# Tile 0's and tile 1's slots chosen anew: load order, ScalarE's slots and the places of VectorE's weight sums

## Chip, cores and metric

One core of a Trainium2 chip. The metric is the device time of one execution in microseconds (us); smaller is better. Times are medians of several executions; all the comparisons below use executions at the full granted clock ("fast"), and where one fell into a throttled state it is said.

## The reference

Eight batches of eight heads of linear attention (576 positions, head size 64), then a mixture of four experts over all 4608 tokens, each expert a product 512 to 1024, a ReLU and a product 1024 to 512, weighted by normalised probabilities.

```python
def phi(x):
    return np.where(x > 0, x, np.exp(x) - 1.0) + 1.0
q_p, k_p = (phi(q), phi(k))
kv = np.einsum('bhsd,bhse->bhde', k_p, v)
z = np.sum(k_p, axis=2)
num = np.einsum('bhsd,bhde->bhse', q_p, kv)
den = np.einsum('bhsd,bhd->bhs', q_p, z)[..., None] + 1e-06
# ... (num / den, heads laid side by side: x)
for e in range(E):
    h = np.maximum(x @ w1[e], 0.0)
    out += p[:, e:e + 1] * (h @ w2[e])
```

## The kernel before

The expert products are done in half-size blocks in the manner of Strassen and Winograd: seven products in place of eight, for which sums of weights, of tokens and of h are needed. The sums of weights are made once, in tile 0 and tile 1, by VectorE, in fp16, 128x1024 each. The sums of h are made in every unit (one tile and one expert) by GpSimd, 128x512 each. The loads go through one queue in the order of a list. Every piece of work has a slot, a number; the slots are sorted and the instructions issued in that order. In the traces here each engine runs its instructions in that order, so a slot decides what stands behind what.

```python
    "DMA": ('w100', 'w101', 'w102', 'w103', 'w200', 'lk1', 'w201', 'w110', 'w111', 'k0', # ... (cut)
    "WS2": ((1.0, 9.5, 29.0, 27.5), (14.5, 32.2, 38.5, 50.9), (70.95, 80.2, 92.75, 79.8), (60.3, 85.95, 92.75, 81.2)),
# ... (cut: weight_sums for w1, slots WS1, L605 to L613, is of the same kind)
    def weight_sums2(e, part):                       # VectorE, both inputs in SBUF: L620, L622, L624, L626
        # ... (cut)
        if part == 0:
            nc.vector.tensor_tensor(out=tw[:, 0], in0=b12, in1=b11, op=AO.subtract)
        elif part == 1:
            nc.vector.tensor_tensor(out=tw[:, 1], in0=b22, in1=tw[:, 0], op=AO.subtract)
        elif part == 2:
            nc.vector.tensor_tensor(out=tw[:, 2], in0=b21, in1=tw[:, 1], op=AO.subtract)
        else:
            nc.vector.tensor_tensor(out=b12, in0=b22, in1=b12, op=AO.subtract)

    def hidden_sum(h, hs, i):                        # GpSimd: L635, L637, L639, L641
        # ... (cut)
        if i == 0:
            nc.gpsimd.tensor_tensor(out=hs[0], in0=a21, in1=a22, op=AO.add)
        elif i == 1:
            nc.gpsimd.tensor_tensor(out=hs[1], in0=hs[0], in1=a11, op=AO.subtract)
        # ... (cut: i == 2 and i == 3 likewise)

    def add_acc(j, e, ns, ps, ds, first):            # frees a PSUM bank that TensorE waits for
        # ... (cut)
        if first:
            nc.scalar.activation(acc, ps, AF.Identity, scale=pscal)             # L568
        else:
            nc.vector.scalar_tensor_tensor(                                      # L570
                out=acc, in0=ps, scalar=pscal, in1=acc, op0=AO.mult, op1=AO.add
            )

    # of the attention of the next batch, on the same PSUM buffers by turns (aps):
    # left_dve (VectorE, L367) reads psum_el and writes qlp; pe_xl (TensorE, L404) then takes that bank as psum_xl;
    # dma_qT (a transposing transfer issued by SyncE) writes qT; nd (TensorE, L465) reads it
# ... (cut)
        for fj, pos in enumerate(CFG["L1P"]):
            put_at(pos, group, fj)
        # ... (cut)
            for i in range(4):
                put_at(CFG["WS1"][e][i], weight_sums, e, i)
                put_at(CFG["WS2"][e][i], weight_sums2, e, i)
        # ... (cut)
        work.sort(key=lambda w: w[0:2])
        for _, _, g in work:
            g[0](*g[1:])
```

Of the kernel before, what the change touches and what calls it, by code (L numbers as in the profile page):

```python
# [17 lines left out]


CFG = {  # L20
    "DMA": ('w100', 'w101', 'w102', 'w103', 'w200', 'lk1', 'w201', 'w110', 'w111', 'k0', 'w120', 'w121', 'v0', 'w210', 'lk0', 'w211', 'lv1', 'k1', 'k2', 'lv0', 'v1', 'w131', 'w130', 'v2', 'k3', 'v3', 'q1', 'q0', 'w220', 'w221', 'q2', 'q3', 'w230', 'w231'),
    "BLK": (-5.0, 2.0, 10.5, 18.5, 28.0, 36.0, 56.0),
    "L1P": (-69.15, -64.1, -39.9, -36.2, -35.4, -24.38, -16.38, -16.08),
    "L2P": ((-14.38, -14.35, -14.33, -13.58, -11.58, -11.51, -11.2, -10.2, -9.5, -4.0, -2.0, 2.45, 2.45, 2.55, 13.55, 16.5), (17.5, 18.7, 18.9, 19.4, 20.95, 21.6, 22.1, 22.2, 26.4, 26.45, 28.55, 30.95, 31.25, 31.3, 34.75, 37.0), (35.75, 38.05, 41.2, 42.0, 43.45, 43.6, 43.6, 43.6, 45.35, 46.05, 47.1, 48.6, 53.95, 55.0, 58.45, 59.1), (54.55, 56.3, 56.4, 58.6, 61.3, 61.4, 63.3, 63.5, 64.1, 64.1, 66.3, 66.89, 70.95, 70.95, 78.25, 78.5)),
    "TS0": (-52.15, -46.1, -23.38, -16.97),
    "WS1": ((-2.0, 1.95, 40.0, 16.05), (-16.88, -10.13, -2.0, -2.2), (7.85, 12.0, 14.95, 10.0), (25.1, 25.38, 33.64, 31.0)),
    "WS2": ((1.0, 9.5, 29.0, 27.5), (14.5, 32.2, 38.5, 50.9), (70.95, 80.2, 92.75, 79.8), (60.3, 85.95, 92.75, 81.2)),
    "ATTN": (
        dict(
            v=(18.3, 24.16, 28.05, 31.12),  # L30
            k=(-2.05, 25.8, 28.0, 28.5),
            kd=(-1.0, 26.5, 29.8, 30.7),
            lv=19.5,
            lk=14.7,
            lkd=15.45,
            kv=(33.8, 34.3),
            q=(34.9, 36.95, 39.2, 41.7),
            qd=(38.25, 38.4, 41.95, 43.6),
            lq=54.05,
            lqd=56.5,  # L40
            qt=(41.6, 43.8, 45.2, 45.4),
            nd=(45.45, 45.55, 46.1, 47.35),
            xt=(50.15, 53.7, 53.95, 55.1),
            qtl=58.23,
            nl=70.95,
            xl=89.22,
            next=(-3.0, -2.05, 33.69, 40.65, 45.2, 45.55),
        ),
        dict(
            v=(4.4, 8.7, 12.1, 14.8),  # L50
            k=(0.3, 2.9, 6.7, 11.25),
            kd=(7.1, 3.84, 14.3, 14.8),
            lv=10.36,
            lk=9.9,
            lkd=11.6,
            kv=(17.5, 19.1),
            q=(20.1, 22.1, 27.0, 30.0),
            qd=(21.75, 27.2, 30.2, 32.3),
            lq=33.9,
            lqd=38.3,  # L60
            qT=35.9,
            nd=(39.3, 40.4, 42.0, 43.5, 45.3, 46.1),
            nl=52.1,
# [3 lines left out]
    "L2ORD": (2, 5, 1, 6, 3, 7, 4),  # L67
    "L2AT": (3.9, 5.0, 5.8, 7.0, 7.2, 8.4, 9.1, 10.3, 12.9, 13.1, 15.1, 15.1, 16.8, 16.8),
    "TSUM": (-6.7, -4.7, -1.6, -0.7),
    "TSUM1": (2.9, 4.1, 6.3, 6.54),  # L70
    "PR": (-20.88, 40.55, 61.5, 52.95),
    "LATE": (4.0, 14.0, 16.0, 24.0),
    "MODE": {'k0': 0, 'q2': 1, 'k3': 0, 'q0': 0, 'k2': 0, 'k1': 1, 'q1': 0, 'q3': 0, 'T3': 0, 'T0': 0, 'T1': 1, 'v1': 2, 'v2': 0, 'v3': 2, 'v0': 0, 'T2': 1},
    "APS": ('s', 'e', 'b', 'py'),
# [953 lines left out]
```

## Time and profile before

| | before |
|---|---|
| time, median of 6 runs (lowest to highest) | 496.37 us (495.51 to 497.09) |
| span of the profiled run, granted clock | 494.2 us, 0.998 |
| TensorE busy, of the span | 483.7 us, 98% |
| VectorE, ScalarE, GpSimd busy | 77%, 68%, 72% |
| time that TensorE's starts lost, by the count of the prediction | 13.13 us, 11.20 of it before 100 us |

"Lost" is how much later a matmul starts than the one before it and its size allow. The prediction below shows the lines of this kernel's profile.

### The profile page before, as it was taken

The page shows a single profiled execution, that of the slowest core. Times are in us where ns is not written, and L with a number is a line of the kernel's source. Part 1 is how long each engine was busy: PE and PEld are TensorE (multiplying, and loading weights), DVE is VectorE, ACT ScalarE, POOL GpSimd, SP SyncE. Part 2 cuts the span into 40 slices and gives each one's busy share as a digit, 9 for nine tenths or more (in the row PEclk, how much of TensorE's full clock was granted, in tenths as well). Part 3 has the DMA queues.
Part 4 walks back from the last instruction along what each step waited for, and adds up shares of the span by engine and source line. Part 5 has one row for each costly group of instructions (what it writes and reads, how often), then busy time and mean ns, then how long its engine had stood idle before and what let it go on. Part 6 is the DMA issues. An engine that isn't in the chain of part 4 may idle for free.

```text
span 494.2 us, 11615 instructions
## 1 busy us (share of the span) xinstructions
PE 483.7 (98%) x4346; PEld 409.7 (83%) x4346; DVE 378.4 (77%) x802; ACT 336.6 (68%) x678; POOL 355.8 (72%) x341
## 2 busy tenths in 40 slices
PE   9999989999999999999999999999999999999996
PEld 4556656788898989898989898989898888888885
DVE  5657888798867987698859886888688756775686
ACT  6767969964987488848894789468954565446530
POOL 3635204778977797769776977698669877987775
PEclk9999999999999999999999999999999999999999
DMA  9999975552355234633466245522231020002003
GB/s 257 213 219 240 272 138 149 184 121 51 108 190 114 57 111 158 137 67 92 134 166 81 71 150 139 102 57 90 87 73 36 4 96 1 1 2 86 1 1 86
DMA packets 82104, 53.65 MB, mean 109 GB/s; under 512 B 46240, under 2 KB 75808, under 8 KB 82048
## 3 DMA queue, kind: packets, MB, share of 16 engines
q1 hardware_dynamic: 70512, 40.00, 31.2%
q0 software_dynamic: 9888, 11.41, 12.2%
q10 hardware_dynamic: 1648, 1.51, 1.1%
q8 instruction: 34, 0.56, 0.5%
q14 instruction: 22, 0.18, 0.1%
HBM read 45.16 MB, written 9.44 MB: 110 GB/s over the span
## 4 chain that ended last, share of the span: by engine, by line
PE 81%; DMA 10%; DVE 3%; ACT 3%; POOL 1%; issue 1%; DVEq 0%; POOLq 0%; ACTq 0%
PE py L668 38%; PE pb L733 22%; PE pe L733 16%; DMA w<-in_moe_w_dram 7%; DMA rawu<-in_q_dram 2%; PE warm_ps L860 1%; PE psum_nd L465 1%; DMA rawb<-in_v_dram 1%; PE psum_kv L425 1%; DVE acc L570 1%; DVE x_sb L448 1%; PE pb L668 1%; PE py L579 0%; ACT u L744 0%; ACT psum_ee L315 0%
## 5 line engine op out<-in xcount | busy, mean ns | idle before, releaser
L570 DVE SCALAR_TENSOR_TENSOR acc<-py,p_sb,acc 128x256 f32<-128x256 f32 (+1 forms) x382 | 182.3, 488 | 49.5 <-PE py L668 40.2
L717 DVE CUSTOM_DVE_ANT_0 h<-pe,u 128x512 f16<-128x512 f32 x140 | 96.3, 688 | 42.1 <-PE pe L733 27.4
L733 PEld LDWEIGHTS <-w 128*128 128x128 f16 x1120 | 108.8, 98 | 17.5 <-issue 1.7
L635 POOL TENSOR_TENSOR hs<-h 128x512 f16<-128x512 f16 x64 | 74.0, 1156 | 55.2 <-DVE h L717 53.8
L668 PEld LDWEIGHTS <-h 128*128 128x128 f16 x1024 | 99.6, 98 | 11.8 <-issue 0.5
L668 PE MATMUL py<-w,h 128*128 128x256 f16 x744 | 106.4, 273 | 0.0
L744 ACT COPY u<-pb 128x512 f32<-128x512 f32 x140 | 82.7, 591 | 27.7 <-PE pb L733 25.5
L637 POOL TENSOR_TENSOR hs<-hs,h 128x512 f16<-128x512 f16 x64 | 74.7, 1168 | 26.7 <-PE py L668 24.1
L733 PEld LDWEIGHTS <-s 128*128 128x128 f16 x840 | 81.6, 98 | 11.8 <-issue 0.4
L733 PE MATMUL pb<-tt,w 128*128 128x256 f16 x560 | 84.0, 273 | 0.9 <-ACT u L744 0.9
L668 PEld LDWEIGHTS <-hs 128*128 128x128 f16 x768 | 74.4, 98 | 9.9 <-issue 1.2
L641 POOL TENSOR_TENSOR hs<-h,hs 128x512 f16<-128x512 f16 x64 | 74.6, 1166 | 3.5 <-PE py L668 2.9
L668 PE MATMUL py<-t,hs 128*128 128x256 f16 x496 | 74.4, 272 | 0.6 <-DVE acc L570 0.4
L639 POOL TENSOR_TENSOR h<-h 128x512 f16<-128x512 f16 x64 | 74.5, 1165 | 0.0
L759 ACT ACTIVATE h<-pe 128x512 f16<-128x512 f32 x70 | 41.8, 597 | 44.9 <-PE pe L733 44.4
L753 ACT COPY pe<-pb 128x512 f32<-128x512 f32 x70 | 40.3, 575 | 41.6 <-PE pb L733 14.7
L777 ACT ACTIVATE h<-pb 128x512 f16<-128x512 f32 x70 | 41.9, 599 | 9.7 <-PE pb L733 9.5
L733 PE MATMUL pb<-tt,s 128*128 128x256 f16 x280 | 42.0, 273 | 0.1
L733 PE MATMUL pe<-tt,s 128*128 128x256 f16 x280 | 42.0, 273 | 0.0
L733 PE MATMUL pb<-xT,w 128*128 128x256 f16 x248 | 37.2, 273 | 0.3 <-DMA w<-in_moe_w_dram 0.2
L733 PE MATMUL pe<-xT,s 128*128 128x256 f16 x248 | 37.2, 273 | 0.1
L668 PE MATMUL py<-w,hs 128*128 128x256 f16 x248 | 37.2, 273 | 0.0
(121 smaller groups left out, 607.1 us busy)
## 6 DMA issues: line engine op xcount, KB each, us to landing
out_dram<-acc SPq DMA_DIRECT2D x32, 256.0 KB, 2.5
w<-in_moe_w_dram POOLq DMA_DIRECT2D x14, 512.0 KB, 13.1
rawb<-in_v_dram SPq DMA_DIRECT2D x26, 256.0 KB, 2.7
rawb<-in_q_dram SPq DMA_DIRECT2D x26, 256.0 KB, 2.7
rawb<-in_k_dram SPq DMA_DIRECT2D x26, 256.0 KB, 3.1
w<-in_moe_w_dram POOLq DMA_DIRECT2D x4, 256.0 KB, 5.8
rawb<-in_k_dram POOLq DMA_DIRECT2D x4, 256.0 KB, 11.5
rl<-in_q_dram SPq DMA_DIRECT2D x16, 64.0 KB, 2.5
```

The costliest lines, as they stand in the source:

```text
L570: nc.vector.scalar_tensor_tensor(out=acc, in0=ps, scalar=pscal, in1=acc, op0=AO.mult, op1=AO.add)
L635: nc.gpsimd.tensor_tensor(out=hs[0], in0=a21, in1=a22, op=AO.add)
L637: nc.gpsimd.tensor_tensor(out=hs[1], in0=hs[0], in1=a11, op=AO.subtract)
L639: nc.gpsimd.tensor_tensor(out=a21, in0=a11, in1=a21, op=AO.subtract)
L641: nc.gpsimd.tensor_tensor(out=hs[3], in0=a12, in1=hs[1], op=AO.subtract)
L668: nc.tensor.matmul(out=ps, lhsT=lhsT(k), rhs=rhs[:, k], start=first and k == 0, stop=k == FH - 1, skip_group_check=True,)
L717: nc.vector._custom_dve(TENSOR_ADD_SAT, out=out, in0=ps, in1=u, s0=BIG, s1=0.0)
L733: nc.tensor.matmul(out=ps[:, kk], lhsT=lk(kc), rhs=rhs[:, kc], start=first and kk == 0 and kc == 0, stop=kc == 1, skip_group_check=True,)
L744: nc.scalar.copy(u, self.b)
L753: nc.scalar.copy(self.e5, self.b)
L759: nc.scalar.activation(self.h[:, :, 0, 0:NH], self.e5, AF.Relu)
L777: nc.scalar.activation(self.h[:, :, 1, 0:NH], self.b, AF.Relu)
```

## The change

Intent: tile 0's and tile 1's slots are chosen anew, so that loads land when they are needed, and VectorE's sums of weights do not fall on GpSimd's sums of h. No instruction is added, removed or resized.

```diff
-    "DMA": ('w100', 'w101', 'w102', 'w103', 'w200', 'lk1', 'w201', 'w110', 'w111', 'k0', 'w120', 'w121', 'v0', 'w210', 'lk0', 'w211', 'lv1', 'k1', 'k2', 'lv0', 'v1', 'w131', 'w130', 'v2', 'k3', 'v3', 'q1', 'q0', 'w220', 'w221', 'q2', 'q3', 'w230', 'w231'),
-    "BLK": (-5.0, 2.0, 10.5, 18.5, 28.0, 36.0, 56.0),
+    "DMA": ('w100', 'w101', 'w102', 'w103', 'k0', 'w201', 'lk1', 'w200', 'w111', 'w110', 'w121', 'w120', 'lv0', 'lk0', 'w211', 'w210', 'v2', 'v1', 'v0', 'k1', 'w130', 'lv1', 'w131', 'q0', 'k2', 'k3', 'v3', 'w220', 'q2', 'q1', 'w221', 'q3', 'w230', 'w231'),
+    "BLK": (-7.0, 0.5, 9.5, 16.5, 27.0, 36.5, 56.0),
...(cut: L1P, L2P, TS0)
-    "WS1": ((-2.0, 1.95, 40.0, 16.05), (-16.88, -10.13, -2.0, -2.2), (7.85, 12.0, 14.95, 10.0), (25.1, 25.38, 33.64, 31.0)),
-    "WS2": ((1.0, 9.5, 29.0, 27.5), (14.5, 32.2, 38.5, 50.9), (70.95, 80.2, 92.75, 79.8), (60.3, 85.95, 92.75, 81.2)),
+    "WS1": ((13.95, 16.35, 48.05, 14.35), (-20.54, -18.83, -3.5, -0.5), (8.8, 8.95, 15.75, 9.75), (24.56, 28.38, 31.14, 25.8)),
+    "WS2": ((-1.55, 8.26, 33.15, 34.42), (19.45, 32.66, 45.5, 63.9), (73.5, 87.35, 91.2, 82.18), (61.8, 93.5, 104.41, 85.13)),
...(cut: the other slots of batch 1's attention)
-            xl=89.22,
+            xl=95.55,
...(cut: TSUM1, PR)
```

More of the change, by code (lines that the diff above doesn't have):

```diff
@@ L20 @@
 CFG = {
-    "DMA": ('w100', 'w101', 'w102', 'w103', 'w200', 'lk1', 'w201', 'w110', 'w111', 'k0', 'w120', 'w121', 'v0', 'w210', 'lk0', 'w211', 'lv1', 'k1', 'k2', 'lv0', 'v1', 'w131', 'w130', 'v2', 'k3', 'v3', 'q1', 'q0', 'w220', 'w221', 'q2', 'q3', 'w230', 'w231'),
-    "BLK": (-5.0, 2.0, 10.5, 18.5, 28.0, 36.0, 56.0),
-    "L1P": (-69.15, -64.1, -39.9, -36.2, -35.4, -24.38, -16.38, -16.08),
-    "L2P": ((-14.38, -14.35, -14.33, -13.58, -11.58, -11.51, -11.2, -10.2, -9.5, -4.0, -2.0, 2.45, 2.45, 2.55, 13.55, 16.5), (17.5, 18.7, 18.9, 19.4, 20.95, 21.6, 22.1, 22.2, 26.4, 26.45, 28.55, 30.95, 31.25, 31.3, 34.75, 37.0), (35.75, 38.05, 41.2, 42.0, 43.45, 43.6, 43.6, 43.6, 45.35, 46.05, 47.1, 48.6, 53.95, 55.0, 58.45, 59.1), (54.55, 56.3, 56.4, 58.6, 61.3, 61.4, 63.3, 63.5, 64.1, 64.1, 66.3, 66.89, 70.95, 70.95, 78.25, 78.5)),
@@ L25 @@
-    "TS0": (-52.15, -46.1, -23.38, -16.97),
-    "WS1": ((-2.0, 1.95, 40.0, 16.05), (-16.88, -10.13, -2.0, -2.2), (7.85, 12.0, 14.95, 10.0), (25.1, 25.38, 33.64, 31.0)),
-    "WS2": ((1.0, 9.5, 29.0, 27.5), (14.5, 32.2, 38.5, 50.9), (70.95, 80.2, 92.75, 79.8), (60.3, 85.95, 92.75, 81.2)),
+    "DMA": ('w100', 'w101', 'w102', 'w103', 'k0', 'w201', 'lk1', 'w200', 'w111', 'w110', 'w121', 'w120', 'lv0', 'lk0', 'w211', 'w210', 'v2', 'v1', 'v0', 'k1', 'w130', 'lv1', 'w131', 'q0', 'k2', 'k3', 'v3', 'w220', 'q2', 'q1', 'w221', 'q3', 'w230', 'w231'),
@@ new lines @@
+    "BLK": (-7.0, 0.5, 9.5, 16.5, 27.0, 36.5, 56.0),
+    "L1P": (-69.15, -64.1, -39.9, -36.2, -35.4, -23.25, -13.43, -13.43),
+    "L2P": ((-13.38, -13.35, -13.33, -12.08, -10.08, -9.81, -9.2, -8.7, -7.5, -5.5, -2.0, -1.45, -0.5, 8.3, 10.35, 12.55), (14.35, 17.2, 17.2, 17.9, 20.95, 21.1, 21.6, 21.7, 28.0, 28.55, 29.05, 31.45, 31.75, 32.5, 34.25, 37.0), (35.75, 37.97, 42.4, 42.55, 43.05, 44.8, 44.8, 45.55, 46.0, 46.55, 46.75, 48.0, 51.75, 58.0, 58.45, 59.1), (54.25, 56.3, 56.89, 58.2, 59.1, 62.1, 63.6, 63.7, 64.1, 65.9, 66.1, 69.0, 69.95, 70.65, 78.45, 78.5)),
@@ L28 @@
+    "TS0": (-52.15, -46.1, -23.38, 1.0),
+    "WS1": ((13.95, 16.35, 48.05, 14.35), (-20.54, -18.83, -3.5, -0.5), (8.8, 8.95, 15.75, 9.75), (24.56, 28.38, 31.14, 25.8)),
+    "WS2": ((-1.55, 8.26, 33.15, 34.42), (19.45, 32.66, 45.5, 63.9), (73.5, 87.35, 91.2, 82.18), (61.8, 93.5, 104.41, 85.13)),
     "ATTN": (
         dict(
-            v=(18.3, 24.16, 28.05, 31.12),
-            k=(-2.05, 25.8, 28.0, 28.5),
-            kd=(-1.0, 26.5, 29.8, 30.7),
-            lv=19.5,
-            lk=14.7,
@@ L35 @@
-            lkd=15.45,
-            kv=(33.8, 34.3),
-            q=(34.9, 36.95, 39.2, 41.7),
-            qd=(38.25, 38.4, 41.95, 43.6),
-            lq=54.05,
-            lqd=56.5,
-            qt=(41.6, 43.8, 45.2, 45.4),
-            nd=(45.45, 45.55, 46.1, 47.35),
-            xt=(50.15, 53.7, 53.95, 55.1),
-            qtl=58.23,
-            nl=70.95,
-            xl=89.22,
-            next=(-3.0, -2.05, 33.69, 40.65, 45.2, 45.55),
+            v=(18.1, 19.16, 22.55, 30.55),
+            k=(-5.5, 26.3, 27.5, 28.5),
@@ new lines @@
+            kd=(0.5, 27.07, 30.0, 30.7),
+            lv=23.45,
+            lk=15.35,
+            lkd=16.3,
+            kv=(33.6, 34.0),
+            q=(36.4, 36.95, 40.2, 43.4),
+            qd=(37.75, 39.0, 40.55, 44.7),
+            lq=54.05,
+            lqd=54.5,
+            qt=(42.1, 45.0, 45.8, 46.25),
+            nd=(46.7, 47.0, 47.05, 47.8),
+            xt=(48.15, 50.45, 51.45, 54.8),
+            qtl=57.23,
+            nl=71.0,
+            xl=95.55,
+            next=(-0.5, 0.5, 36.3, 44.55, 46.65, 47.45),
@@ L69 @@
     "TSUM": (-6.7, -4.7, -1.6, -0.7),
-    "TSUM1": (2.9, 4.1, 6.3, 6.54),
-    "PR": (-20.88, 40.55, 61.5, 52.95),
+    "TSUM1": (3.76, 4.1, 6.3, 9.92),
+    "PR": (-21.88, 47.0, 56.27, 39.85),
     "LATE": (4.0, 14.0, 16.0, 24.0),
```

## The prediction

> **What bounds the kernel now.** I read the page first, then the time by stages, then TensorE's own timeline, and only then the waits. The stage table (window; its length; busy us and instruction count of PE, PEld, DVE, ACT, POOL; granted clock; share of the DMA engines; GB/s) says most:
>
> ```profile
> 0.00:20.00 20.00, 18.46 (x120) 9.75 (x121) 14.12 (x41) 13.14 (x28) 11.04 (x23) 1.00 1.09 240
> 20.00:60.00 40.00, 38.21 (x258) 23.91 (x257) 26.35 (x48) 31.29 (x62) 15.81 (x23) 1.00 1.17 241
> 60.00:75.00 15.00, 13.65 (x110) 8.60 (x109) 12.88 (x31) 10.26 (x22) 0.99 (x2) 1.00 0.73 142
> 75.00:115.00 40.00, 39.10 (x340) 31.24 (x338) 34.51 (x65) 33.37 (x74) 26.39 (x23) 1.00 0.55 147
> 115.00:480.00 365.00, 365.00 (x3446) 328.35 (x3444) 280.91 (x599) 248.08 (x496) 293.22 (x265) 1.00 0.32 83
> ```
>
> From 115 to 480 us TensorE has no gap. Only tile 0 and the entry into tile 1 can give time back. Busy time flatters TensorE, because the modelled end of a matmul lies some 0.16 us behind the start of the next. So I took starts instead: a 256-column matmul is followed by the next after 109 ns, a 512-column one after 216, a 130-column one after 56, a 128-column one after 55 (medians of the timeline). Whatever a start lies later than that is lost. The loss is 13.1 us in all: 2.9 before 10 us, 1.0 in 10 to 20, **7.8 us in 20 to 120**, about 0.02 per 10 us from there to 480, and 0.6 at the end. The 7.8 us is the whole purse of this change: the order of the first 170 matmuls (up to about 29 us) and of everything from tile 2 on is the same in both kernels.
>
> Who took the 7.8 us (lines of TensorE's timeline: start, us, what, idle time before it and what ended it):
>
> ```profile
> 41.82 0.60 PE L733 MATMUL pb<-tt,w 128*128 128x256 f16 x4 [0.31 <-ACT u L744]
> ...
> 56.78 0.61 PE L579 MATMUL py<-w,h 128*128 128x512 f16 x2 [0.47 <-DMA w<-in_moe_w_dram]
> ...
> 67.10 0.27 PE L465 MATMUL psum_nd<-kvz,qT 128*128 128x130 f16 x2 [0.38 <-ACT qT L416]
> 67.53 0.29 PE L465 MATMUL psum_nd<-kvz,qT 128*128 128x130 f16 x2 [0.15 <-DVE x_sb L448]
> 68.11 0.29 PE L465 MATMUL psum_nd<-kvz,qT 128*128 128x130 f16 x2 [0.30 <-DVE x_sb L448]
> ...
> 98.12 0.60 PE L668 MATMUL py<-t,hs 128*128 128x256 f16 x4 [0.35 <-DVE acc L570]
> ```
>
> By starts: 2.9 us in seven waits before 60 us (ScalarE copies 0.56 and 0.47, the landings of w130 0.41 and w220 0.63, sums and kp on VectorE 0.26, 0.27, 0.33); 2.5 us in 65 to 72 us, where q arrives late and TensorE then waits for each numerator (1.05 us for the copies of qT, 1.44 us for x_sb); 2.1 us in 84 to 112 us; the rest in pieces under 0.1 us.
>
> The sums that the title means are seen on VectorE and on GpSimd:
>
> ```profile
> 93.45 1.46 DVE L626 TENSOR_TENSOR w<-w 128x1024 f16<-128x1024 f16 x1
> 94.84 1.64 DVE L622 TENSOR_TENSOR t<-w,t 128x1024 f16<-128x1024 f16 x1
> 96.40 0.68 DVE L626 TENSOR_TENSOR w<-w 128x1024 f16<-128x1024 f16 x1
> ```
> ```profile
> 93.22 1.15 POOL L639 TENSOR_TENSOR h<-h 128x512 f16<-128x512 f16 x1
> 94.33 1.60 POOL L641 TENSOR_TENSOR hs<-h,hs 128x512 f16<-128x512 f16 x1
> ```
>
> The same sum takes 0.68 us alone and 1.46 or 1.64 us where GpSimd is adding.
>
> **What the Trainium skill says.** "SBUF — State Buffer", section "Who interferes with whom", says that a VectorE instruction with two SBUF inputs takes its second one through the interface that GpSimd reads by, and that the one that issues second is blocked until the first has ended. The trace agrees in kind: the pair above costs VectorE 0.78 and 0.96 us and GpSimd 0.45. The accumulations (one input in PSUM) beside GpSimd keep to 0.47 us. "Perfetto Trace Analysis", section "Identifying the Most-Contended Engine", warns that matmul busy time is no measure of TensorE's headroom; the trace agrees (98% on the page, yet 7.8 us to be had in the first quarter). "DMA: Bandwidth & Descriptors", section "Issuing engines are not separate DMA queues", says that transfers of all issuers share the same engines. Here the queue is full from 14 to 68 us (share over 1), so a new order moves landings without adding bandwidth.
>
> **The change part by part.** No instruction is added, removed or resized: every engine has the same work, and GpSimd's list gets only another order of DMA issues. So the gain is only a matter of waits.
>
> *1. Weight sums away from the sums of h.* In the profile before, four VectorE sums are stretched: 0.92, 1.46, 1.64 and 1.64 us instead of 0.68, together 2.9 us; four GpSimd sums take 1.50, 1.60, 1.48 and 1.60 instead of 1.15, together 1.6 us. Most is off the path. What TensorE lost behind it: 0.52 and 0.12 us at 98 to 99 us (an accumulation queued behind the sums of 93.45 to 97.08), 0.30 at 107.55 (it waited for GpSimd's L639) and 0.12 at 111.5: 1.06 us. In the new order these sums stand apart, and the third sum of expert 3's w2 goes from second in a pair to some 10 us later. I count 0.7 us gained.
>
> *2. The order of the loads.* A 512 KB piece of weights lands 2.5 us after the one before it, a 256 KB piece of q or k after 0.7. New: k0 before w20x, w201 before w200, w111 before w110. Before, w110 landed at 27.55 us and w111 at 30.13, and the first product of expert 1, which reads w110, started at 29.62. Now w110 is the last of this group, and k0 (0.65) is ahead of it: 30.13 + 0.65 = 30.8 us, against a use at 29.65: **1.15 us lost**, new. w200 comes at 25.07 + 0.7 = 25.8, just when layer 2 begins (25.73). This replaces the 0.26 us at 31.6.
>
> *3. Later landings.* The set of pieces up to w121 is equal, so it ends at 35.6 in both. Then w130 comes by about 47.2 (before 50.00), so its wait of 0.41 goes. q1 moves behind w220, so w220 lands by about 55.3 to 56 (before 56.74) and its 0.63 goes. q2 lands by 56 (before 61.66), the last q by 60.5 to 61.5 (before 62.39).
>
> *4. Slots of ScalarE and of expert 1's blocks.* The blocks come closer together, with more TensorE work between a sixth product and the seventh, which needs ScalarE's copy. Of the 0.56 and 0.47 I leave 0.3. k0 to k3 and the last v still tie kv: 0.5 as before. Sum to 57 us: 1.15 + 0.1 + 0.3 + 0.5, with small pieces 2.2 us; before, the start at 57.23 lay 2.96 us behind a run without waits. Gain 0.75.
>
> *5. The passage at 65 to 72 us.* ScalarE is full in 50 to 65 us. Two v casts and one k go earlier, and it no longer waits for q2 (0.55 us before). Of the 1.05 us for qT I leave 0.5 to 0.7. The numerators then stay a chain: eight steps of a reciprocal and a product (0.55 us each) through two PSUM banks, with less TensorE work between them than before (0.9 us against 1.3 in 4 us). I leave 1.9 us where there were 1.44. Net here about 0.
>
> Sum: 0.75 + 0 + 0.7 = 1.45 us, and a little for pieces under 0.1 us: 1.7 us, of 496.5 to **494.8 us**.
>
> **Rivals.** (a) *The new wait for w110 is carried to the end.* For it: it is a landing, which nothing on chip hastens. Against: a delay at 30 us uses up the later waits for landings. If it stays whole and the passage at 65 gets worse, the time is 496.5 to 497.5. (b) *ScalarE is the bound at 75 to 100 us.* It is busy 4.9 of each 5 us there, with the same work in nearly the same order, so an earlier start hits it as new waits for its copies: gain under 0.5 us, 496 us. (c) *All waits for landings and sums vanish.* Without the 7.8 us it would be 488.7; half of it gives 492.6. (d) *The sums are all of it*: 1.06 us, 495.5.
>
> **Range and chances.** Even the whole purse, 7.8 us, is 1.6%: over 2% faster is shut out unless the steady part changes, whose order doesn't. Slower by 2% would need 9.9 us of new waits, and the largest I find is 1.15. So within 2% is nearly certain. The range, 492.6 to 497.0, goes from half of the purse to rival (a).
>
> **What would show it.** Right: VectorE's 128x1024 sums all near 0.68 us and GpSimd's near 1.15; a wait for a landing of w just before the first product of expert 1 near 30 us; none for w near 50 and 56 us; the waits of psum_nd for x_sb still there, about 1.9 us; no change after 120 us except an earlier start. Wrong: stretched sums still there, no wait at 30 us (then the gain is nearer 2.5 us), or new waits for ScalarE's u in 75 to 100 us.

## The result, and the profile after

| | before | after |
|---|---|---|
| time, median of 6 runs | 496.37 us (495.51 to 497.09) | 496.31 us (495.56 to 497.18) |
| span of the profiled run | 494.2 us | 494.7 us |

The ratio is 1.0000, with a 95% interval of 0.9985 to 1.0015: the same. A ratio here is the mean time of one kernel's fast runs over that of the other's fast runs of the same rounds, so it isn't quite the ratio of the medians quoted.

The stages of the changed kernel, with the columns of the table in the prediction:

```profile
0.00:20.00 20.00, 17.63 (x119) 9.38 (x120) 14.06 (x41) 12.89 (x28) 10.90 (x23) 1.00 1.07 245
20.00:60.00 40.00, 38.44 (x264) 24.64 (x262) 27.26 (x48) 31.59 (x63) 16.01 (x23) 1.00 1.18 237
60.00:75.00 15.00, 13.68 (x108) 8.03 (x107) 12.75 (x31) 10.64 (x22) 1.58 (x3) 1.00 0.73 147
75.00:115.00 40.00, 38.74 (x342) 31.41 (x341) 34.97 (x65) 33.03 (x73) 26.72 (x22) 1.00 0.56 150
115.00:480.00 365.00, 364.41 (x3438) 327.56 (x3436) 280.72 (x596) 247.68 (x495) 292.45 (x264) 1.00 0.31 82
```

TensorE does 264 matmuls in 20 to 60 us where it did 258, so it is ahead there; in 75 to 115 us its busy time falls from 39.10 to 38.74 us, and the steady part has 0.6 us less than its 365. The losses by stretch say it more exactly (us, one profile each):

| stretch | before | after | gained |
|---|---|---|---|
| 0 to 20 | 3.92 | 4.12 | -0.20 |
| 20 to 60 | 2.97 | 2.20 | 0.77 |
| 60 to 80 | 2.56 | 2.94 | -0.38 |
| 80 to 100 | 1.75 | 0.50 | 1.25 |
| 100 to 120 | 0.50 | 1.75 | -1.25 |
| 120 to 160 | 0.07 | 0.74 | -0.67 |
| 160 to the end | 1.36 | 1.38 | -0.02 |
| sum | 13.13 | 13.63 | -0.50 |

By 100 us the changed kernel is 1.44 us ahead, about what was predicted. The next 20 us take 1.25 us of it. Not every row is the order's doing: in 0 to 20 us four kernels with the same order there lose 3.75 to 4.36 us, and most of the 0.67 us of 120 to 160 us is one wait that other runs do not show at that size (after_again, below). So the sum of -0.50 is not a result; the medians of the times differ by 0.06 us the other way. TensorE's timeline of the changed kernel (start, us, what, idle time before it and what ended it) shows where:

```profile
31.44 0.61 PE L733 MATMUL pb<-xT,w 128*128 128x256 f16 x4 [0.95 <-DMA w<-in_moe_w_dram]
...
67.88 0.29 PE L465 MATMUL psum_nd<-kvz,qT 128*128 128x130 f16 x2 [0.26 <-DVE x_sb L448]
68.43 0.29 PE L465 MATMUL psum_nd<-kvz,qT 128*128 128x130 f16 x2 [0.26 <-DVE x_sb L448]
...
106.10 0.34 PE L465 MATMUL psum_nd<-kvz,qT 128*128 128x130 f16 x3 [0.42 <-DMA qT<-qp]
107.13 0.27 PE L404 MATMUL psum_xl<-identh,x_sl 128*128 128x128 f16 x2 [0.69 <-DVE qlp L367]
...
117.40 1.03 PE L668 MATMUL py<-t,h 128*128 128x256 f16 x8
...
149.55 0.60 PE L668 MATMUL py<-w,h 128*128 128x256 f16 x4 [0.50 <-ACT acc L568]
```

The first is the predicted new wait for w110 (1.11 us by starts); the two of 67.88 and 68.43 are the passage that was to stay. New and not predicted are the landing of qT at 106 us (0.59 by starts), psum_xl at 107 us (0.85), and 0.26 at 117 us. qT is read by the matmuls of the numerators of attention, psum_nd. The kernel before enters the same numerator later, and without a wait:

```profile
107.08 0.33 PE L465 MATMUL psum_nd<-kvz,qT 128*128 128x130 f16 x3
```

Now VectorE and GpSimd of the changed kernel around it (start, us, instruction):

```profile
97.22 0.68 DVE L626 TENSOR_TENSOR w<-w 128x1024 f16<-128x1024 f16 x1
...
99.15 0.73 DVE L622 TENSOR_TENSOR t<-w,t 128x1024 f16<-128x1024 f16 x1
99.81 0.67 DVE L322 SCALAR_TENSOR_TENSOR qp<-qp,psum_ee 128x512 f16<-128x512 f16 x1
...
102.62 1.06 DVE L624 TENSOR_TENSOR t<-w,t 128x1024 f16<-128x1024 f16 x1
104.07 0.69 DVE L717 CUSTOM_DVE_ANT_0 h<-pe,u 128x512 f16<-128x512 f32 x1 [0.40 <-ACT acc L568]
104.68 1.67 DVE L622 TENSOR_TENSOR t<-w,t 128x1024 f16<-128x1024 f16 x1
106.28 0.47 DVE L570 SCALAR_TENSOR_TENSOR acc<-py,p_sb,acc 128x256 f32<-128x256 f32 x1
106.67 0.40 DVE L367 SCALAR_TENSOR_TENSOR qlp<-qlp,psum_el 128x256 f16<-128x256 f16 x1
```
```profile
99.29 1.61 POOL L639 TENSOR_TENSOR h<-h 128x512 f16<-128x512 f16 x1
100.86 1.16 POOL L641 TENSOR_TENSOR hs<-h,hs 128x512 f16<-128x512 f16 x1
101.97 1.15 POOL L635 TENSOR_TENSOR hs<-h 128x512 f16<-128x512 f16 x1
103.20 1.49 POOL L637 TENSOR_TENSOR hs<-hs,h 128x512 f16<-128x512 f16 x1
104.65 1.16 POOL L639 TENSOR_TENSOR h<-h 128x512 f16<-128x512 f16 x1
105.76 1.60 POOL L641 TENSOR_TENSOR hs<-h,hs 128x512 f16<-128x512 f16 x1
```

The weight sums still meet GpSimd: four VectorE sums are stretched (1.07, 1.54, 1.06, 1.67 us) where four were before (0.92, 1.46, 1.64, 1.64), and six GpSimd sums instead of four. The reading is simple once the ends are compared. GpSimd's sum of 104.65 ends at 105.81; VectorE's sum, issued 0.03 us after it, ends at 106.35, which is 0.54 later. The sum of 102.62 ends 0.56 after GpSimd's end of 103.12. The other way about, the sum of 99.15 began before GpSimd's of 99.29: VectorE took 0.73, and GpSimd paid, ending 1.01 after VectorE. The ten profiles at full clock with such sums have 29 stretched VectorE sums, and each ends 0.54 to 0.55 us after the end of the GpSimd sum that was running (0.68 us alone); their 41 stretched GpSimd sums end 1.01 to 1.02 us after the end of the VectorE sum (1.15 alone). So the one that comes second waits for nearly the whole of the other. The Trainium skill says in "SBUF — State Buffer", section "Who interferes with whom", that two-input VectorE instructions contend with GpSimd's reads, and that such contention is an exclusive lock; these ends agree: it is a wait, not a slower pace.

Behind the stretched L622 of 104.68 stand two things in VectorE's order that TensorE needs: an accumulation and qlp, which holds the PSUM bank of psum_xl. That suggested the first theory. The transfer of qT has a sum in front of it as well: it is issued (100.56) when VectorE has made the last part of qp (99.81), and that part stands straight behind the sum of 99.15.

### The profile page after: what moved, and what is told of

It is laid out like the page before. It is cut to its first block, busy times and chain, and to the rows that moved or that the text cites. A ratio compares the mean times of both kernels' runs of the same rounds, so it can differ in the third digit from the quotient of the medians.

```text
span 494.7 us, 11609 instructions
## 1 busy us (share of the span) xinstructions
PE 482.6 (98%) x4346; PEld 409.2 (83%) x4346; DVE 379.8 (77%) x802; ACT 336.4 (68%) x678; POOL 356.4 (72%) x341
## 4 chain that ended last, share of the span: by engine, by line
PE 83%; DVE 5%; DMA 5%; ACT 4%; POOL 1%; issue 1%; SPq 0%; ACTq 0%; DVEq 0%
PE py L668 37%; PE pb L733 23%; PE pe L733 17%; PE py L579 3%; DMA w<-in_moe_w_dram 3%; DVE acc L570 2%; PE psum_kv L425 1%; DMA rawb<-in_v_dram 1%; DVE x_sb L448 1%; PE psum_nd L465 1%; DVE h L717 1%; ACT qp L310 1%; POOL w L183 1%; DMA rawh<-in_q_dram 1%; ACT psum_ee L315 1%
## 5 line engine op out<-in xcount | busy, mean ns | idle before, releaser
L568 ACT ACTIVATE acc<-py,p_sb 128x256 f32<-128x256 f32 (+1 forms) x68 | 32.9, 497 | 6.9 <-PE py L579 2.7
L733 PE MATMUL pe<-xT,w 128*128 128x256 f16 x248 | 37.2, 273 | 0.3 <-ACT pe L753 0.3
```

Source lines behind the costliest of these rows:

```text
L733: nc.tensor.matmul(out=ps[:, kk], lhsT=lk(kc), rhs=rhs[:, kc], start=first and kk == 0 and kc == 0, stop=kc == 1, skip_group_check=True,)
```

## The experiments

Twelve kernels ran. All results were correct except the two that are wrong on purpose. Theory A: the 1.25 us are lost because what VectorE owes TensorE stands behind a sum that met GpSimd. Rivals: the slot of psum_xl alone is at fault; the gain of 80 to 100 us would have been stopped by the landing of qT anyway; the wait for w110 is carried to the end. A loss by stretch is read from one profile. The changed kernel was not in the rounds of e1 to e8, so those times are set against the kernel before, and against the changed kernel only by way of it, which leaves some 0.9 us either way.

### The slot of psum_xl back to its old place

```diff
-            xl=95.55,
+            xl=89.22,
```

> The changed kernel with one slot put back: the transposes of the rows left over (psum_xl) stand before the first numerators of batch 2, as before the change (xl 89.22 in place of 95.55). Theory A (what was gained by 105 us was lost in waits that the new order itself makes): the wait of 0.85 us of psum_xl at 107 us is gone, TensorE stands about 0.8 us earlier from there on, and the time is 0.4 to 0.9 us below the changed kernel, near 495.6. Rival B (something after 120 us, such as the landing of the stores at 149 us, sets the time whatever comes before): the wait at 107 us goes, another at 110 to 150 us grows by as much, and the time is within 0.2 us of the changed kernel.

Measured (e1_xl_early): 495.91 us, ratio to the kernel before 1.0003 (0.9992 to 1.0014). The wait for psum_xl is gone, but the losses in 100 to 120 us are 1.72 us after 1.75. TensorE's timeline of this kernel:

```profile
105.90 0.34 PE L465 MATMUL psum_nd<-kvz,qT 128*128 128x130 f16 x3 [0.47 <-DMA qT<-qp]
106.44 0.60 PE L668 MATMUL py<-t,hs 128*128 128x256 f16 x4 [0.20 <-DVE acc L570]
117.02 1.03 PE L668 MATMUL py<-t,h 128*128 128x256 f16 x8 [0.36 <-DVE acc L570]
```

The rest of the wait went to the next thing that VectorE owed, an accumulation behind the same L622 (1.56 us here). So by the profile the slot of psum_xl is not the cause; at most it chooses which instruction shows the wait. The theory A of this text, a time 0.4 to 0.9 us lower, did not come; what came is the pattern of its rival B: one wait goes, and others grow by as much (0.36 us new at 106, 0.52 after 0.26 at 117).

### w110 ahead of w111

```diff
-'w200', 'w111', 'w110', 'w121',
+'w200', 'w110', 'w111', 'w121',
```

> The changed kernel with w110 loaded before w111. Both theories: w110 lands near 28.9 instead of 31.4 us, so the wait of 1.1 us for it falls to under 0.2, and w111 costs at most 0.5. Theory A: TensorE is 0.6 to 1.0 us earlier at 55 us, but most of that is given back at 60 to 70 us, where q and ScalarE's copies of qT come no earlier; 0 to 0.4 us remain at the end. Rival (a delay at 30 us is carried whole): 0.6 to 1.0 us remain.

Measured (e2_w110_first): 495.84 us, 1.0000 (0.9987 to 1.0013). The wait of 1.11 us at 31.4 is gone. Of it 0.67 us is left by 80 us (losses in 20 to 80: 4.47 after 5.14), because 0.44 us net comes back in small waits (0.22 and 0.18 us for sums, 0.24 and 0.57 for landings at 41 and 61 us, while 0.49 at 26 and 0.27 at 62 us go). 100 to 120 us loses 1.75 again, and no more: so in the profile the 0.67 us is kept to the end, as the rival had it. The times do not show it, but an interval of 0.13% either way, some 0.6 us, could hide it. So w110 costs what was said; what taking it away gives at the end is not settled by this run.

### Only the new slots of the weight sums, in the kernel before

```diff
 (the kernel before, with the WS1 and WS2 lines of the kernel after, nothing else)
```

> The kernel before, with only the slots of the weight sums (WS1, WS2) taken from the change. If the placement of the sums is what the change is good for: VectorE's 128x1024 sums after 75 us are all near 0.68 us and the time falls by 0.7 us or more. Theory A (the slots are relative, so the sums still meet GpSimd, which is busy nine tenths of the time from 85 to 109 us): at least three sums are still over 0.9 us, and the time is within 0.7 us of the kernel before, either way.

Measured (e3_sums_only): 497.52 us, 1.0037 (1.0025 to 1.0049): 1.8 us slower than the kernel before, where theory A had allowed 0.7. Four sums are stretched here too (0.86, 1.56, 0.94, 1.56 us). The new slots bring no gain by themselves; 0.56 us is lost at 34.3 and 0.89 at 41.0 us, where TensorE waits for VectorE's w and h behind sums that now come earlier, and the waits for qT, an accumulation and again an accumulation at 108 to 119 us are there as well. The slots of the sums were fitted to the new places of the blocks, so this run doesn't measure them in their own surroundings; it does show that they do not stand apart from GpSimd.

### No weight sums in the late stretch (wrong results on purpose)

```diff
     def weight_sums2(e, part):
         w, tw = w2_sb[e], t2_sb[e]
+        if e >= 2:
+            if part < 3:
+                # ... (cut: tw[:, part] from two halves of w1_sb[0] instead)
+            return
 ...
-                put_at(CFG["WS2"][e][i], weight_sums2, e, i)
+                put_at(CFG["WS2"][e][i] if e < 2 else -21.0, weight_sums2, e, i)
```

The eight w2 sums of experts 2 and 3 leave the stretch after 60 us. Six are replaced early by sums of weights that are there already, two are left out, so the result is wrong (relative error 1.67). The same was done to the kernel before (slot -20.5).

> Wrong result on purpose: the changed kernel with the eight sums of w2 of experts 2 and 3 taken out of the time after 75 us (six of them made from other data at 20 to 30 us, where VectorE idles, the two in place left out). It bounds all that these sums and their meetings with GpSimd can cost. Theory A: no stretched sum of VectorE or of GpSimd is left, the wait of psum_xl at 107 us falls from 0.85 to under 0.3, the wait for the landing of qT (0.59) stays or grows, and the time falls by 0.5 to 1.2 us. If the meetings cost what the title supposes: more than 1.5 us. Rival B: under 0.3 us.

> Wrong result on purpose: the kernel before with the same eight late sums taken out as in e4_no_late_sums. It measures what the sums and their meetings cost the kernel before; the prediction counted 1.06 us of TensorE's waits for the meetings alone (at 98, 99, 107.55 and 111.5 us). If that count was right: those four waits gone and the time 0.8 to 1.4 us below the kernel before. If an earlier TensorE meets the landing of qT instead: that wait appears, 0.3 us or more, and the gain is 0.3 to 0.7 us.

Measured for the changed kernel (e4_no_late_sums): 494.50 us, 0.9972 (0.9960 to 0.9983). No sum is stretched; 100 to 120 us loses 0.21 instead of 1.75 us, of which 0.15 is qT. For the kernel before (e8_before_no_late_sums): 494.73 us, 0.9989 (0.9977 to 1.0000); its losses in 80 to 120 us fall from 2.25 to 0.97. So the sums in the late stretch cost the kernel before 1.3 us in the profile, whose run is the fastest of the five, and some 0.6 us in the times (means of 494.93 and 495.57). They cost the kernel after more: 1.5 us in its profile, and 0.28% (1.4 us) in the times, set against the kernel before. Both texts missed in part. In the kernel before the four waits that the prediction named are gone and the wait for qT is 0.17 us, as the first reading had it, but the time fell by less than its 0.8 us; in the kernel after the wait for qT did not stay. So the term that the prediction counted (1.06 us behind the sums, 0.7 to be had) was there in the profile, and the change did not collect it. These two runs take away the sums with their meetings, and do not tell the one from the other. Nor is qT a fixed bound, for with nothing behind a sum the same landing costs 0.15 us.

### All late sums but one moved to places without GpSimd

```diff
-(73.5, 87.35, 91.2, 82.18), (61.8, 93.5, 104.41, 85.13)),
+(40.5, 44.6, 54.4, 65.2), (61.8, 68.9, 100.0, 85.13)),
```

> The changed kernel with seven of the late sums of w2 put where the trace shows GpSimd idle: two of expert 2 in VectorE's idle time at 61 and 63 us, one at 73, the one in place at 81, one of expert 3 at 83, one at 110; same instructions, same result. Contention (the meetings, not the sums themselves, delay what VectorE owes TensorE at 100 to 120 us): no sum after 75 us above 0.8 us, the waits of 0.85 (psum_xl) and 0.26 us (accumulation at 117) gone, and a time 0.7 to 1.3 us below that of the changed kernel and of the kernel before. Rival (VectorE's load, not the meetings): the sums only crowd VectorE at 60 to 85 us, new waits there, and the time is within 0.3 us.

Measured (e5_sums_apart; six slots are changed, not seven as the text says): 496.90 us, 1.0021 (1.0009 to 1.0034), slower than the kernel before where 0.7 to 1.3 us faster was expected, in two groups: two runs at 495.4 to 495.6 (the profiled one among them) and four at 496.8 to 497.3. No profile of the second group exists, and it stays unexplained. In the profile only one sum is left stretched, the one that I placed badly (slot 100.0, at 111.6 us), and TensorE pays 0.86 and 0.18 us behind it. The psum_xl wait is gone. No sum stands in front of the last part of qp any more, and the wait for qT is 0.34 us in place of 0.59.

> As e5_sums_apart, and w110 loaded before w111. If the 0.7 us that e2_w110_first kept at 80 us (4.5 us lost by 80 us against 5.1) is carried once the waits at 107 us are out of its way: 1.2 to 2.0 us below the kernel before. If the landing of qT at 106 us is a floor: the wait there grows to over 1.0 us and e6 is not more than 0.3 us below e5.

The same with w110 ahead of w111 (e6_apart_w110): 495.26 us (494.93 to 496.88), 1.0002 (0.9990 to 1.0013). The waits at 113.7 and 115 us are unchanged. Neither forecast came: the time is not 1.2 us below the kernel before, and the wait for qT did not grow to 1.0 us, it is 0.24.

> As e6_apart_w110, with the first numerators of batch 2 behind one more group of TensorE work (39.9 in place of 39.3, for this batch alone), and psum_xl back in front of them. The wait for the landing of qT falls by 0.44 us, one group. Expected 0.3 to 0.5 us below e6 if that landing is the next bound; no difference if VectorE's accumulations are.

The same (e7_apart_nd_later), with `xl=89.22` and batch 2's first numerator at slot 39.9 in place of 39.3, so that TensorE has other work while qT lands: 494.98 us (494.61 to 496.63), 0.9998 (0.9985 to 1.0010); the mean is 0.26 us below e6's with a standard error of 0.47, so the forecast of 0.3 to 0.5 is not tested by the times. The wait for qT is gone; the badly placed sum is the one thing left in 100 to 120 us. TensorE, VectorE and GpSimd of this kernel there:

```profile
113.63 0.60 PE L668 MATMUL py<-w,hs 128*128 128x256 f16 x4 [0.70 <-DVE acc L570]
```
```profile
111.31 1.27 DVE L624 TENSOR_TENSOR t<-w,t 128x1024 f16<-128x1024 f16 x1
112.51 0.68 DVE L717 CUSTOM_DVE_ANT_0 h<-pe,u 128x512 f16<-128x512 f32 x1
113.11 0.47 DVE L570 SCALAR_TENSOR_TENSOR acc<-py,p_sb,acc 128x256 f32<-128x256 f32 x1
```
```profile
110.89 1.15 POOL L637 TENSOR_TENSOR hs<-hs,h 128x512 f16<-128x512 f16 x1 [0.82 <-PE py L668]
112.00 1.60 POOL L639 TENSOR_TENSOR h<-h 128x512 f16<-128x512 f16 x1
```

It is the same pattern as at 104.7 us in the kernel after: a sum that waits for GpSimd's end (112.04, then 0.54 us), h and an accumulation behind it, TensorE behind these.

### One sum, one numerator, and the idle slot

The last four ran together, on one chip in the same rounds. The first is the changed kernel once more.

> The changed kernel itself, unaltered, so that the three others of this call have it on the same chip in the same rounds. Expected: 496.0 us within 0.6, ratio to the kernel before 1.000 within 0.0015; stretched sums at 92.6 and 104.7 us again, TensorE's waits at 106 (landing of qT) and 107 us (psum_xl) again. If the wait of 0.66 us at 149.5 us (ScalarE's L568, which waits for the landing of a store) is there again at that size, it belongs to the kernel; if it is 0.3 us or less, it is jitter of that one profile.

Measured (after_again): fast runs 495.12 to 496.66 us, mean 496.10; ratio 1.0002 (0.9983 to 1.0020). Its profiled run was throttled (clock 0.949, 507.38 us), so its waits are not compared; the stretched sums at 93.0 and 105.3 us are there again. The wait of 0.66 us at 149.5 us of the first profile is most likely no part of the order: it is 0.28 in e1_xl_early, 0.12 in e2_w110_first, 0.34 in e11_one_sum_nd_later, 0.21 in e8_before_no_late_sums, and absent in e3 to e6 and in e10_one_sum. ScalarE waits there for the landing of a store, 4.4 us after its issue in that profile and 3.0 in the kernel before. A second profile at full clock of the changed kernel itself does not exist.

One slot of the changed kernel moved, the L622 of 104.68 us:

```diff
-(61.8, 93.5, 104.41, 85.13)),
+(61.8, 68.9, 104.41, 85.13)),
```

> The changed kernel with one slot moved: the second w2 sum of expert 3 (L622, 1.67 us at 104.7 us) goes some 25 us earlier. Theory A (what VectorE owes TensorE stands behind this one stretched sum): the waits at 107.1 (psum_xl, 0.85 us) and 117.4 us (0.26) go; if qT still lands at 106 us that wait stays and may grow to 0.6 to 1.0 us, because nothing else holds TensorE up; time 0.3 to 1.0 us less than the changed kernel in these rounds. Theory B (the landing of qT hides behind it, so that a VectorE free of the sum gives nothing): the psum_xl wait goes, the qT wait grows by as much, time equal within 0.2 us.

Measured (e10_one_sum): mean 495.47 (median 495.50), 0.63 us less than the changed kernel of the same rounds, with a standard error of 0.31, so not clear of noise; 0.9989 to the kernel before (0.9974 to 1.0004). VectorE now goes straight through what it owes, and TensorE waits for qT alone:

```profile
104.43 0.69 DVE L717 CUSTOM_DVE_ANT_0 h<-pe,u 128x512 f16<-128x512 f32 x1 [0.39 <-ACT acc L568]
105.04 0.47 DVE L570 SCALAR_TENSOR_TENSOR acc<-py,p_sb,acc 128x256 f32<-128x256 f32 x1
105.43 0.41 DVE L367 SCALAR_TENSOR_TENSOR qlp<-qlp,psum_el 128x256 f16<-128x256 f16 x1
```
```profile
106.56 0.34 PE L465 MATMUL psum_nd<-kvz,qT 128*128 128x130 f16 x3 [0.53 <-DMA qT<-qp]
```

The wait for psum_xl (0.85 us) is gone, the one for qT went from 0.59 to 0.69, so most of what was freed is kept in the profile, where 100 to 120 us loses 1.00 in place of 1.75: by the profile theory A holds, and the landing alone would not have taken the gain. The run moves the sum as a whole, its own 0.68 us with the 0.99 us of the meeting, and no run keeps the one without the other in that place. An estimate from the lines of the changed kernel: without the 0.99 us qlp would have ended at 106.08 in place of 107.07, and TensorE, which came for its bank at 106.28, would not have waited; so the meeting is enough for the 0.85 us. What I expected wrongly is the 0.26 us at 117 us, which stays: the sum in front of that accumulation (L624 at 115.9) takes 0.68 us; it came first, and GpSimd's sum paid (1.53 us). So there the sum costs TensorE by its own length.

The same with the numerator's slot at 39.9:

```diff
-                batch_steps(bts[j + 1], nxt, put, ATTN[j > 0], ATTN[1])
+                batch_steps(bts[j + 1], nxt, put, dict(ATTN[1], nd=(39.9,) + ATTN[1]["nd"][1:]) if j == 1 else ATTN[j > 0], ATTN[1])
```

> The kernel of e10_one_sum with the first numerator of batch 2 two blocks' pieces later (slot 39.9), so that TensorE has other work while qT lands. Theory A: no wait for qT and none for psum_xl in 100 to 112 us, loss in 100 to 120 us under 0.5 us instead of 1.75; time 0.8 to 1.4 us below the changed kernel (494.8 or so). Theory B expects the same here, so this run against e10_one_sum tells them apart. A third (everything gained before 105 us is taken again further on by VectorE's or ScalarE's own work): the waits move to 112 to 120 us and the time stays at 496.

Measured (e11_one_sum_nd_later): mean 495.01 (median 494.89), 1.09 us less than the changed kernel (standard error 0.42) and 0.46 less than e10_one_sum (0.33, not clear of noise); 0.9979 (0.9959 to 0.9998). The wait for qT is 0.19, the losses in 100 to 120 us are 0.61 after 1.75 in the changed kernel (0.5 or less was expected: 0.37 us is left at 116.4, behind that same L624). So in its profile the changed kernel, with two slots moved, keeps most of what it had gained by 100 us.

Last, e7_apart_nd_later with its bad sum in VectorE's idle time before 104 us:

```diff
-(40.5, 44.6, 54.4, 65.2), (61.8, 68.9, 100.0, 85.13)),
+(40.5, 44.6, 54.4, 65.2), (61.8, 68.9, 91.2, 85.13)),
```

> The kernel of e7_apart_nd_later with the last badly placed sum (L624 of expert 3, 1.27 to 1.54 us at 111 us) moved to 102.5 us, into the 1.36 us in which VectorE waits for ScalarE anyway. It meets GpSimd there and will still take over 1.0 us. Theory A (a stretched sum costs only where VectorE owes TensorE something behind it): the waits at 113.6 and 115.1 us (1.04 us) go though the sum is still stretched; time 494.0 us within 0.5, ratio to the kernel before 0.9975 within 0.001. Rival (being stretched is what costs, wherever it stands, because GpSimd's sum is stretched too and TensorE waits for that): new waits for hs of GpSimd at 104 to 108 us, time as e7_apart_nd_later, 495.0 us.

Measured (e9_apart_idle_slot): five fast runs of 493.36 to 495.10 us, median 493.80 and mean 493.95; ratio to the kernel before 0.9958 (0.9940 to 0.9977), to the changed kernel of the same rounds 493.95 / 496.10 = 0.9957. It beats both kernels, by 2 us. The gain is somewhat more than expected (0.9975 within 0.001). Its profiled run was throttled (clock 0.851, 559.82 us); there TensorE is slow, the moved sum (111.85, 0.68 us) comes first and it is GpSimd's sum behind it that is stretched (111.95, 1.60 us). So it is shown that the order with the sum in this place is the faster one, but not that the sum is stretched there and costs nothing. The step from e7_apart_nd_later (0.9998, in other rounds) is about twice the 1.04 us of waits that were to go, and the rest is not explained. Nor are the parts of the 2 us told apart: this kernel has the order of w110, six sums, psum_xl and the numerator changed. The rival's time (495.0 us) did not come; its waits for hs could not be looked for at full clock.

## Why the prediction was right or wrong

The time was predicted at 494.8 us in 492.6 to 497.0; 496.31 is inside the range and "within 2%" was right, but of the gain of 1.7 us nothing came, and the prediction's own sign of being wrong, "stretched sums still there", did. That the time fell inside the range is luck: the range reached up to 497.0 for rival (a), which is not what the profile shows. By its steps:

1. *Weight sums away from the sums of h, 0.7 us: failed.* The step said that in the new order these sums stand apart. They do not: four are stretched as before. The four waits that the step named (1.06 us) did go, but 1.70 us of new ones came in their place at 106 to 117 us (0.59, 0.85, 0.26); losses in 80 to 120 us are 2.25 us in both kernels. The size of what could be had was right in the profile (1.28 us in the kernel before when the sums are taken out; 0.6 in the times), the mechanism of a meeting too; what failed is the reading of an order as a time. I saw that the sums had other neighbours on VectorE and took this for distance from GpSimd. In the kernel after, GpSimd has three gaps of over 0.1 us between 84.8 and 107.4 us (0.24, 0.83 and 1.02 us), room for two sums of 0.68 us: of six weight sums in that stretch one (97.22) fell into a gap, one (99.15) came 0.14 us ahead of GpSimd, and four were caught. That could have been counted from the profile of the kernel before, where GpSimd has four such gaps (0.89, 1.83, 0.73, 0.22 us) in the 23.6 us from 85.0 to 108.6. What a sum costs TensorE is then decided by what stands behind it: the 0.85 us at 107 us went when that one sum was moved (e10_one_sum, in the profile).
2. *The order of the loads: right but for w200.* w110 landed at 31.40 us (predicted 30.8), and its wait is 1.11 us (1.15). w200 landed at 26.39, with a wait of 0.49 us where about 0.1 was left for it.
3. *Later landings: right.* w130 landed at 46.93 (47.2), w220 at 54.79 (55.3 to 56), the last q at 61.48 (60.5 to 61.5), and the waits for w are gone.
4. *Slots of ScalarE and of the blocks: right in the sum, by luck in part.* The stretch from 20 to 60 us gained 0.77 us, for 0.75, but errors cancel in it: w200 cost 0.49 us for 0.1 and ScalarE's copies 0.56 for 0.3 (0.44 of it at 32.8 us, for another copy than the two named), while kv cost nothing for 0.5. From 40 to 60 us nothing is lost (under 0.05 us).
5. *The passage at 65 to 72 us: right, with 0.4 us more around it.* Four waits for x_sb of 0.42 us each stay, with one of 0.14 (1.84 us for 1.9). From 60 to 80 us the loss is 2.94 after 2.56: net 0 was predicted.

Rival (a), the wait for w110 carried to the end, is not what took the gain: by 100 us the changed kernel is 1.44 us ahead with that wait in it. Whether the wait itself is carried stays open: without it the profile keeps 0.67 us to the end, and the times show nothing (e2_w110_first). Rival (b), ScalarE, did not come: 80 to 100 us loses 0.5 us. A cause that no rival named is the landing of qT. The transfer is issued 0.98 us earlier in the changed kernel (100.56 after 101.54) but lands only 0.36 earlier. The same transfer in the lists of transfers of before, and then of after (size of a group, us from issue to landing):

```profile
qT<-qp SPq DMA_TRANSPOSE x1, 4.9
```
```profile
qT<-qp SPq DMA_TRANSPOSE x1, 5.5
```

It was hidden as long as TensorE was late. A weight sum has its part in this too, though it is not stretched: the sum of 99.15 us (0.73 us) stands in front of the last part of qp, on which the transfer waits. In the profiles where that sum is moved or left out the wait for qT is 0.34 us (e5), 0.24 (e6) and 0.15 (e4); in e10_one_sum, which keeps it, it is 0.69. No run moves that sum alone. That the numerator can be put behind the landing is shown by e11_one_sum_nd_later (0.19 us left).

Open: the second group of times of e5_sums_apart; why e3_sums_only loses in 20 to 80 us as much as it does; why e8_before_no_late_sums gained half in the times of what its profile shows; why the transfer of qT takes 4.9 us in the kernel before and 5.5 to 6.0 in all others; and how e9_apart_idle_slot looks at full clock.

## What to carry to other kernels

Before you count a gain from "these two no longer meet", list the gaps of the busier one: an engine that is 90% busy in a stretch has few gaps to aim at, and a new order will meet it again. By these profiles a meeting costs TensorE what is owed behind it, so put the instruction that may be stretched where its engine waits anyway, not in front of an accumulation whose PSUM bank is awaited, nor in front of what a transfer waits for. Issued first it goes through in its own time (0.73 us at 99.15), but the other engine then pays (1.61 us for 1.15). And a gain upstream of a landing can be lost at that landing: look at what holds up its issue, and at whether its reader has other work to do first.

## What the Trainium skill lacked or had wrong

- "SBUF — State Buffer", section "Who interferes with whom", has the lock but no sizes for two-input instructions. The runs show them: 29 stretched 128x1024 fp16 sums end 0.54 to 0.55 us after GpSimd's sum ends (alone they take 0.68), 41 GpSimd sums of 128x512 end 1.01 to 1.02 us after VectorE's (alone 1.15). The first to come pays little: the VectorE sum of 99.15 took 0.73.
- "Perfetto Trace Analysis", section "Identifying the Most-Contended Engine", warns of matmul busy time and names other measures, but none that counts what TensorE's starts lose. Start-to-start time less the spacing of that size did it here: 13.13 us in the kernel before, of a span of 494.2, each part with its place and its cause.
- "DMA: Bandwidth & Descriptors", section "DMA Transpose (X-bar)", gives constraints and no time from issue to landing; the one of qT took 4.9 us in the kernel before, 5.5 in the one after, and 5.5 to 6.0 in the profiles of the experiments.
